# A recurrent scan with a soft mixture of experts: slot sums divided behind the experts, gates by sigmoid where the table allows, a new written order

## The chip, the cores and the metric

The kernel runs on one core of one Trainium2 chip. Such a core has a matrix engine (TensorE, PE in the profile), a vector engine (VectorE, DVE), an engine for functions of single elements (ScalarE, ACT), a general one (GpSimd, POOL) and a queue engine (SyncE, SP) from which this kernel issues all its transfers. Every engine works through its own list of instructions in order; semaphores hold an instruction back until what it needs is there. The metric is the device time of one execution in microseconds (us). PSUM, the memory into which TensorE writes, has eight banks of 128 rows by 512 numbers of four bytes here; all other tiles lie in SBUF.

## The reference

Four sequences of 5056 tokens with 256 channels go through a gated linear recurrence, and its output, as 20224 tokens, through a soft mixture of 8 experts with 4 slots each. Cut to what matters:

```python
# recurrence (B=4, S=5056, D=256), c = 8
sig_r, sig_i = sigmoid(r_gate), sigmoid(i_gate)
a_t  = exp(c * sig_r * log(clip(sigmoid(a_param), 1e-6, 1 - 1e-6)))
norm = sqrt(maximum(1 - a_t * a_t, 1e-6))
u    = norm * sig_i * x
h[t] = a_t[t] * h[t-1] + u[t]            # y = all h
# soft mixture of experts over the N = 20224 rows of y
logits = y @ phi                         # (N, 32): 8 experts x 4 slots
d = exp(logits - logits.max(0)); d /= d.sum(0) + 1e-9
slot_in = d.T @ y                        # (32, 256)
for e in range(8):                       # F = 1024
    slot_out[e] = maximum(slot_in[e] @ w1[e], 0) @ w2[e]
c = exp(logits - logits.max(1)); c /= c.sum(1) + 1e-9
out = c @ slot_out                       # (N, 256)
```

The softmax of `d` runs over all tokens, so no slot is complete before the last token has been scanned, and no output row exists before the experts are done.

## The kernel before, in words

**Windows and units.** The tokens are cut into 40 windows of 512 (the last has 256). The windows are grouped into 21 units, of one window at the start, then of two (`UNITS`, line 16). What ScalarE does on 2048 columns at once it does for a unit.

**The front of a window.** SP loads the r gate, the i gate and x (L368), tokens on the rows. TensorE turns the r gate channel-major (L383, two halves of 128 channels); ScalarE takes tanh(r/2) of each half (L393) and, for the unit, the sigmoid of the i gate (L405). GpSimd multiplies it with x (L412). Two exponentials for each unit, one for each half, make the decay a (L425): the sigmoid of r is (1 + tanh(r/2))/2, so exp(8 L sig(r)) is exp(4L tanh + 4L), and `ca`, the column with 4L (L is the logarithm of the clipped sigmoid of `a_param`), stands as scale and as bias. GpSimd squares a (L433); ScalarE takes the root of 1 minus that (L440). TensorE turns i·x channel-major (L450); VectorE multiplies it with the root (L460) and scans (L473, one for each half, each taking the last column of the window before). TensorE turns y token-major (L493), and VectorE or ScalarE copies it (L281 in the one case, L279 in the other) into one of six y tiles.

**Groups of four windows.** TensorE makes the logits (L539); VectorE copies them and takes the running maximum (L548 to L552); ScalarE makes the correction exp(old maximum - new maximum) (L557); TensorE turns logits minus maximum token-major (L563, L566), ScalarE takes their exponential (L572), TensorE multiplies it with y and a column of ones (L581, so the 257th column holds the sum of weights), and VectorE folds the result into `accS` with the correction (L590 for the first group, L592 for the others). Each of the four windows of a group has its own 32 rows of `accS`.

**From the scans to the slots.** The four row blocks have maxima of their own. L621 to L638 bring their common maximum back to the rows, L643 and L646 make the weights, L649 puts them on a pattern of identities (`Wt`). Two products then add the four blocks up (L656), and a third (L657) adds up the sums of weights, repeated on all 128 rows. VectorE adds 1e-9, takes the reciprocal and multiplies (L662 to L664): that is `slotT`, the normalised slots.

**Experts, tokens, stores.** Four pairs of experts go through L713 (first product), a copy, L725 (transposition), L731 (maximum with 0) and L740 (second product, all summed into one bank). The result is copied to `soS`, multiplied with the pattern of identities (L762), which repeats the 32 slot rows four times, and copied to `soR`. The token side makes the softmax of the logits over the slots (L790 to L810), turns it (L814), multiplies it with `soR` (L839, 32 rows at a time), copies the result (L279, L281) and stores it (L856). The expert weights come over the same SP queue (L691, L694).

**What sets the order.** All this is written as operations with a key, an engine, an estimated duration and the keys that they need. The table `ORDER` (line 25) lists the operations' numbers, a `b` marking the second of two possible engines. `Plan.order()` goes through it, books each operation on its engine by the estimated durations, and places every buffer at that point: `Plan.take` gives it one of 38 halves of 19 G pairs, six y tiles, two e tiles and eight banks, preferring what is free by the estimated times. The instructions are then emitted in the table's order. So the estimated durations order nothing by themselves, but they decide which buffer an operation gets, and thereby on what it waits.

**Tables.** ScalarE holds one table of functions at a time: exponential with tanh, sigmoid with tanh, square root, or logarithm with exponential. A function of another table makes it load one (ACT_TABLE_LOAD). The planner books 1.283 us for it (`TABLE_US`) and keeps the name of the table loaded.

## Time and profile before

| what | value |
|---|---|
| median of 3 runs | 308.71 us (307.37 to 308.96) |
| the profiled execution | 307.92 us |
| its span (first to last instruction) | 306.1 us |
| granted TensorE clock, mean | 0.928 |
| TensorE busy | 241.1 us (79%) |
| VectorE busy | 238.0 us (78%) |
| ScalarE busy | 246.1 us (80%) |
| GpSimd busy | 181.7 us (59%) |
| moved over the DMA queues | 100.03 MB, mean 327 GB/s |

How to read it: the page gives busy time by engine, then the span in 40 slices with the busy share of each engine in tenths, then the DMA queues, the chain of work that ended last, and the costliest groups of instructions. A row of a timeline reads: start, duration, engine, source line, operation, out<-in, shape, count; in brackets the idle time of the engine before it and what ended that idle time. A row of a group reads: line, engine, operation, count, then busy us and the mean of one in ns, then the idle time before the group's instructions. Lines (L440) are lines of the kernel.

### The profile page before, as it was taken

Reading aid. Unit: us, or ns where it says so; the run is one execution under the profiler, and the core shown is the slowest. Engines: PE = TensorE matmul, PEld = TensorE weight load, DVE = VectorE, ACT = ScalarE, POOL = GpSimd, SP = SyncE. Lnnn points to the kernel's source line nnn. Section 1 sums busy time; section 2 is a strip of 40 time slices with the busy share of each in tenths; the row PEclk is TensorE's granted clock in tenths of the full one; section 3 lists DMA queues with packets and bytes.
Section 4 is the critical chain, followed back from the end, with each engine's and each line's share of the span. In section 5 each row is a group of like instructions: output and inputs, shape, how many; then the busy total and the mean of one; then the engine's idle time right before and its main releaser. Section 6 shows DMA issues by size and latency. Waiting matters only on the chain.

```text
span 306.1 us, 5779 instructions
## 1 busy us (share of the span) xinstructions
PE 241.1 (79%) x2134; PEld 170.0 (56%) x2134; DVE 238.0 (78%) x370; ACT 246.1 (80%) x311; POOL 181.7 (59%) x121
## 2 busy tenths in 40 slices
PE   3605797969888896988989788878999999898900
PEld 3604665737646754766577464736563677656700
DVE  0003999699999998999999989979967869975600
ACT  5999999999999999999999999997220457874320
POOL 1389986988598899699599996991000241031000
PEclk9955999999999999799999999999999999995565
DMA  7999999967998993998856997999990019999996
GB/s 252 415 405 408 408 376 412 396 255 286 399 383 323 410 365 122 378 413 281 327 207 238 384 363 305 335 385 349 406 359 6 2 60 401 405 403 407 361 409 269
DMA packets 28032, 100.03 MB, mean 327 GB/s; under 512 B 3362, under 2 KB 3364, under 8 KB 28004
## 3 DMA queue, kind: packets, MB, share of 16 engines
q1 hardware_dynamic: 28004, 99.66, 84.8%
q8 instruction: 17, 0.28, 0.4%
q14 instruction: 11, 0.09, 0.1%
HBM read 78.94 MB, written 20.71 MB: 326 GB/s over the span
## 4 chain that ended last, share of the span: by engine, by line
PE 25%; ACT 25%; DVE 15%; issue 9%; POOL 6%; DMA 3%; ACTq 0%; SPq 0%; DVEq 0%; POOLq 0%
PE b L839 7%; ACT g L425 7%; DVE g L473 6%; ACT g L393 5%; DVE b L460 4%; ACT g L405 4%; POOL g L412 3%; ACT g L440 3%; POOL g L433 2%; DVE y L281 2%; PE b L713 2%; PE b L740 2%; PE b L493 2%; PE b L450 2%; ACT y L279 2%
## 5 line engine op out<-in xcount | busy, mean ns | idle before, releaser
L412 POOL TENSOR_TENSOR g<-g,g 128x1024 f32<-128x1024 f32 (+1 forms) x40 | 92.7, 2347 | 10.6 <-ACT g L405 10.1
L433 POOL TENSOR_TENSOR g<-g 128x1024 f32<-128x1024 f32 (+1 forms) x40 | 73.8, 1873 | 25.0 <-ACT g L425 21.9
L460 DVE SCALAR_TENSOR_TENSOR b<-g,b 128x512 f32<-128x512 f32 (+1 forms) x80 | 51.5, 677 | 31.4 <-ACT g L440 30.2
L450 PE MATMUL b<-ident,g 128*128 128x128 f32 x316 | 47.6, 286 | 21.7 <-POOL g L412 15.5
L493 PE MATMUL b<-ident,g 128*128 128x128 f32 x316 | 46.9, 283 | 10.4 <-DVE g L473 4.1
L450 PEld LDWEIGHTS b<-ident,g 128*128 128x128 f32 x316 | 35.8, 145 | 34.1 <-POOL g L412 17.7
L383 PE MATMUL b<-ident,g 128*128 128x128 f32 x316 | 46.5, 288 | 8.1 <-DMA g<-in_r_gate_dram 3.2
L473 DVE TENSOR_TENSOR_SCAN g<-g,g,b 128x512 f32<-128x512 f32 x40 | 50.3, 1271 | 0.2
L473 DVE TENSOR_TENSOR_SCAN g<-g,b 128x512 f32<-128x512 f32 (+7 forms) x46 | 49.2, 1094 | 0.3
L493 PEld LDWEIGHTS b<-ident,g 128*128 128x128 f32 x316 | 35.1, 143 | 23.7 <-DVE g L473 8.6
L425 ACT ACTIVATE g<-g,ca 128x1024 f32<-128x1024 f32 (+2 forms) x44 | 47.5, 1158 | 0.0
L810 POOL TENSOR_TENSOR y<-y,rs 128x512 f32<-128x512 f32 x10 | 10.4, 1048 | 61.3 <-DVE rs L807 59.8
L383 PEld LDWEIGHTS b<-ident,g 128*128 128x128 f32 x316 | 36.4, 146 | 18.0 <-ACT g L393 4.3
L393 ACT ACTIVATE g<-b 128x512 f32<-128x512 f32 x80 | 42.2, 605 | 2.5 <-PE b L383 2.4
L281 DVE COPY y<-b 128x512 f32<-128x512 f32 x55 | 36.4, 678 | 6.9 <-PE b L814 3.5
L405 ACT ACTIVATE g<-g 128x2048 f32<-128x2048 f32 (+2 forms) x22 | 38.2, 1755 | 0.1
L440 ACT ACTIVATE g<-g 128x2048 f32<-128x2048 f32 (+2 forms) x22 | 37.2, 1736 | 0.1
L279 ACT COPY g<-b 128x512 f32<-128x512 f32 x47 | 24.7, 593 | 14.3 <-PE b L839 13.5
L839 PE MATMUL b<-soR,y 32*128 32x256 f32 x320 | 31.2, 462 | 3.4 <-DVE y L281 2.3
L839 PEld LDWEIGHTS b<-soR,y 32*128 32x128 f32 x320 | 22.0, 219 | 10.0 <-ACT g L279 3.2
L281 DVE COPY g<-b 128x512 f32<-128x512 f32 x33 | 21.0, 680 | 5.1 <-PE b L839 4.8
L279 ACT COPY y<-b 128x512 f32<-128x512 f32 x34 | 18.7, 592 | 5.9 <-PE b L493 5.9
(83 smaller groups left out, 244.0 us busy)
## 6 DMA issues: line engine op xcount, KB each, us to landing
g<-in_x_dram SPq DMA_DIRECT2D x39, 512.0 KB, 6.7
g<-in_i_gate_dram SPq DMA_DIRECT2D x39, 512.0 KB, 8.1
out_dram<-g SPq DMA_DIRECT2D x39, 512.0 KB, 6.2
g<-in_r_gate_dram SPq DMA_DIRECT2D x38, 512.0 KB, 6.6
g<-in_moe_w_dram SPq DMA_DIRECT2D x32, 512.0 KB, 6.3
g<-in_r_gate_dram SPq DMA_DIRECT2D x3, 256.0 KB, 5.8
g<-in_i_gate_dram SPq DMA_DIRECT2D x1, 256.0 KB, 8.9
g<-in_x_dram SPq DMA_DIRECT2D x1, 256.0 KB, 8.8
```

The costliest lines, as they stand in the source:

```text
L281: nc.vector.tensor_copy(out=dst, in_=srct)
L383: nc.tensor.transpose(out=by_tile(rp, n)[:, j, :], in_=rows(("r", w), n)[:, j, h * P : (h + 1) * P], identity=ident,)
L393: nc.scalar.activation(halves(("A", w))[:, h, :c], Bk(("rp", w, h))[:, :c], AF.Tanh, scale=0.5)
L405: nc.scalar.activation(a, a, AF.Sigmoid)
L412: nc.gpsimd.tensor_tensor(out=rows(("x", w), n), in0=rows(("i", w), n), in1=rows(("x", w), n), op=ALU.mult)
L425: nc.scalar.activation(a, a, AF.Exp, scale=ca[:, h : h + 1], bias=ca[:, h : h + 1])
L433: nc.gpsimd.tensor_tensor(out=halves(("N", w))[:, :, :c], in0=a, in1=a, op=ALU.mult)
L450: nc.tensor.transpose(out=by_tile(up, n)[:, j, :], in_=rows(("x", w), n)[:, j, h * P : (h + 1) * P], identity=ident,)
L460: nc.vector.scalar_tensor_tensor(up, halves(("N", w))[:, h, :c], 1e-3, up, op0=ALU.max, op1=ALU.mult)
L473: nc.vector.tensor_tensor_scan(dst, dst, up[:, s0:s1], init, op0=ALU.mult, op1=ALU.add)
L493: nc.tensor.transpose(out=yp[:, j, h * P : (h + 1) * P], in_=halves(("A", w))[:, h, (2 * i + j) * P : (2 * i + j + 1) * P], identity=ident,)
L839: nc.tensor.matmul(Bk(("op", w0, n))[:, i * D : (i + 1) * D], hT()[r, (2 * i2 + i) * P : (2 * i2 + i + 1) * P], soR[r, :], start=True, sto ...
```

## The change

**Slot sums.** The third product at L657 is gone. `slotT` is now a plain copy of the two sums, not normalised. The maximum with 0 and the two products of an expert go through with a positive factor on a slot, so the division can stand behind them. A new operation `dn` makes four products of 32 by 1 (`Wt` with the column of sums of weights), so that the denominator of a slot stands in a column, on the rows on which the slot outputs are after the identity product; `rd` adds 1e-9 to it and takes the reciprocal, and the copy to `soR` becomes a scaling by that column, on whichever engine has it.

**Gates.** Where the planner finds the sigmoid table loaded for all gates of a unit, `plain` is true: the gate is then sigmoid(r) in place of tanh(r/2), and the exponential has `ca8`, a new column with 8L, as scale and no bias. With the new table of the order this is so for units 6, 8, 10, 14, 22 and 26 (by their first window); these hold 24 of the 80 gates and 12 of the 44 exponentials. All others keep their form.

**PSUM tiles and costs.** The list of eight one-bank tiles is renamed (`bank` to `banks`). Several estimated durations are new, and the accumulating products of the second half of a y tile now name the copy of the first half beside that of the second.

**Order.** The table is another one, with two operations more.

```diff
 ORDER = """
-1 74 96 5 33 11 115 55 13 12 34 56 75 116 4 35 219 137 57 241 97 159 301 76 138 160 98 179 201 117 2 0 6 7 8 9
...
+1 74 96 5 115 2 0 3 6 7 8 9 10 77 79 101 99 118 78 102 80 100 119 120 83 121 11 16 14 15 33 55 36 58 124 17 60
...
-            o.start, o.end = t, t + us
+            o.start, o.end, o.table = t, t + us, table
...
-    bank = [ps.tile([P, C], F32, name=f"b{i}") for i in range(8)]
+    banks = [ps.tile([P, C], F32, name=f"b{i}") for i in range(8)]
...
+    ca8 = const.tile([P, H], F32, name="ca8")
...
-    rd = const.tile([P, 1, NS], F32, name="rd")
+    rd = const.tile([P, 1], F32, name="rd")
...
     def e_decay3(o):
+        nc.vector.tensor_scalar(ca8, ca, 8.0, None, op0=ALU.mult)
         nc.vector.tensor_scalar(ca, ca, 4.0, None, op0=ALU.mult)
...
+    def plain(unit):
+        return all(plan.by_key[("sr", v, h)].table == "S" for v in unit for h in range(H))
...
-            op(("L" + nm, w), "DMA", (2.6 if (nm, w) == ("i", 0) else 1.29) * f, load(nm), alloc=gets(nm), uses=has(nm))
+            op(("L" + nm, w), "DMA", 1.29 * f, load(nm), alloc=gets(nm), uses=has(nm))
...
-                nc.scalar.activation(halves(("A", w))[:, h, :c], Bk(("rp", w, h))[:, :c], AF.Tanh, scale=0.5)
+                f, k = (AF.Sigmoid, 1.0) if plain(unit) else (AF.Tanh, 0.5)
+                nc.scalar.activation(halves(("A", w))[:, h, :c], Bk(("rp", w, h))[:, :c], f, scale=k)
...
-                    nc.scalar.activation(a, a, AF.Exp, scale=ca[:, h : h + 1], bias=ca[:, h : h + 1])
+                    if plain(unit):
+                        nc.scalar.activation(a, a, AF.Exp, scale=ca8[:, h : h + 1])
+                    else:
+                        nc.scalar.activation(a, a, AF.Exp, scale=ca[:, h : h + 1], bias=ca[:, h : h + 1])
...
             op(("acc", t, j), "PE", 0.48, e_acc(j),
-               deps=[("ee", t), ("acc", t, j - 1)] + [("yc", w, j // 2) for w in ws],
+               deps=[("ee", t), ("acc", t, j - 1)] + [("yc", w, i) for w in ws for i in {0, j // 2}],
...
     def sp():
-        return Bk(("sp",))[:, : (H + 1) * NS].rearrange("p (h s) -> p h s", s=NS)
+        return Bk(("sp",))[:, : H * NS].rearrange("p (h s) -> p h s", s=NS)
...
-        nc.tensor.matmul(
-            sp()[:, H, :], accS[:, D : D + 1].broadcast_to([P, P]), Wt, start=True, stop=True
-        )
 
     def e_slot(o):
-        nc.vector.tensor_scalar(rd, sp()[:, H : H + 1, :], 1e-9, None, op0=ALU.add)
+        nc.vector.tensor_copy(out=slotT, in_=sp())
+
+
+    def e_dn(o):
+        for j in range(J):
+            nc.tensor.matmul(
+                Bk(("dn",))[32 * j : 32 * j + NS, :1], Wt, accS[:, D : D + 1], start=True, stop=True
+            )
+
+    def e_rd(o):
+        nc.vector.tensor_scalar(rd, Bk(("dn",))[:, :1], 1e-9, None, op0=ALU.add)
         nc.vector.reciprocal(rd, rd)
-        nc.vector.tensor_tensor(out=slotT, in0=sp()[:, :H, :], in1=rd.broadcast_to([P, H, NS]), op=ALU.mult)
...
     def e_s2(o):
-        copy(o, soR, Bk(("sr",))[:, :D])
+        if o.on == "ACT":
+            nc.scalar.activation(soR, Bk(("sr",))[:, :D], AF.Copy, scale=rd)
+        else:
+            nc.vector.tensor_scalar(soR, Bk(("sr",))[:, :D], rd, None, op0=ALU.mult)
...
-    op(("s2",), ("DVE", "ACT"), {"DVE": 0.34, "ACT": 0.28}, e_s2, deps=[("s1",)], uses=[("sr",)])
+    op(("s2",), ("DVE", "ACT"), {"DVE": 0.34, "ACT": 0.28}, e_s2, deps=[("s1",), ("rd",)], uses=[("sr",)])
```

In the lists that follow, `g`, `y`, `e` and `b` with a number are the G halves, y tiles, e tiles and banks as the planner placed them; `m`, `n`, `d` are running maxima, their negatives and the corrections, `rm` the maxima over a token's slots. Lines after the change are those of the new file, some 5 to 20 higher.

ScalarE, the fourth of the seven stretches that take square roots. Before (L440 root, L279 copy of y, L405 sigmoid):

```order
L425 ACTIVATE g_64<-g_64,ca 128x2x512 x2
L440 ACT_TABLE_LOAD
L440 ACTIVATE g_79<-g_79 128x2048
L279 COPY y_81<-b_95 128x2x256
L440 ACTIVATE g_65<-g_65 128x2048
L279 COPY y_85<-b_89 128x2x256
L279 COPY y_81<-b_93 128x2x256
L279 COPY y_82<-b_90 128x2x256
L279 COPY y_83<-b_94 128x2x256
L440 ACTIVATE g_73<-g_73 128x2048
L405 ACT_TABLE_LOAD
L405 ACTIVATE g_68<-g_68 128x2048
```

The same stretch after the change (L449 root, L280 copy, L411 sigmoid, L566 correction factor, L400 gate):

```order
L566 ACTIVATE d_145<-m_122,n_134 128x1
L280 COPY y_81<-b_91 128x2x256
L400 ACTIVATE g_71<-b_88 128x512
L449 ACT_TABLE_LOAD
L449 ACTIVATE g_74<-g_74 128x2048
L449 ACTIVATE g_67<-g_67 128x2048
L449 ACTIVATE g_62<-g_62 128x2048
L280 COPY y_83<-b_93 128x2x256
L411 ACT_TABLE_LOAD
L411 ACTIVATE g_73<-g_73 128x2048
```

The three roots stand behind each other, two copies of y stand here in place of five, one of them ahead of the table load with a correction and a gate.

VectorE where the slots are made. Before (L592 folds a group in, L649 the weights, L662 to L664 the slots, L796 the first step of the token side):

```order
L592 SCALAR_TENSOR_TENSOR accS<-accS,d_150,b_94 128x257
L592 SCALAR_TENSOR_TENSOR accS<-accS,d_152,b_90 32x257
L649 SCALAR_TENSOR_TENSOR Wt<-R,wj 128x32
L592 SCALAR_TENSOR_TENSOR accS<-accS,d_151,b_88 96x257
L662 TENSOR_SCALAR rd<-b_91 128x32
L663 RECIPROCAL rd<-rd 128x32
L664 TENSOR_TENSOR slotT<-b_91,rd 128x64
L796 TENSOR_REDUCE rm_155<-b_88 128x16
```

After (L640 the common maximum, L652 and L658 the weights, L601 the folding in, L668 the slots, L816 the token side):

```order
L816 TENSOR_REDUCE rm_158<-b_92 128x16
L640 TENSOR_REDUCE mmax<-b_95 1x32
L601 SCALAR_TENSOR_TENSOR accS<-accS,d_151,b_90 128x257
L652 TENSOR_TENSOR wj<-m_130,b_93 128x1
L658 SCALAR_TENSOR_TENSOR Wt<-R,wj 128x32
L601 SCALAR_TENSOR_TENSOR accS<-accS,d_152,b_89 96x257
L601 SCALAR_TENSOR_TENSOR accS<-accS,d_153,b_91 32x257
L668 COPY slotT<-b_91 128x64
L816 TENSOR_REDUCE rm_156<-b_93 128x16
```

The slots take one instruction in place of three, and the weights stand ahead of two foldings in place of one.

TensorE behind the experts. Before (L740 second product of the experts, L814 a transposition of the token side, L762 the product with the identities, L790 the next token transposition, L839 the first store product):

```order
L740 MATMUL b_90<-g_73,g_74 32x256 x4
L740 MATMUL b_90<-g_68,g_74 32x256 x4
L740 MATMUL b_90<-g_63,g_74 32x256 x4
L814 MATMUL b_91<-ident,y_84 128x128 x4
L762 MATMUL b_90<-soS,R 128x256
L790 MATMUL b_94<-ident,l_102 128x4x32 x4
L839 MATMUL b_95<-soR,y_84 128x256
```

After (L757, L834, L779, L810 and L859 are those lines; L673 is the denominator):

```order
L757 MATMUL b_92<-g_70,g_62 32x256 x4
L757 MATMUL b_92<-g_69,g_62 32x256 x4
L757 MATMUL b_92<-g_61,g_62 32x256 x4
L673 MATMUL b_90<-accS,Wt 32x1 x4
L834 MATMUL b_91<-ident,y_83 128x128 x4
L779 MATMUL b_92<-soS,R 128x256
L810 MATMUL b_90<-ident,l_102 128x4x32 x4
L859 MATMUL b_91<-soR,y_83 128x256
L859 MATMUL b_92<-soR,y_83 128x256
```

The four products of the denominator stand between the last expert's product and the transposition, and the first store products have other banks.

More of the change, by code (lines that the diff above doesn't have):

```diff
@@ L73 @@
+1140 1214 1192 1207 1141 1147
 """
@@ L228, in Bk @@
     def Bk(key):
-        return bank[plan.place[key]]
+        return banks[plan.place[key]]
     def rows(key, n):
@@ L399, in window @@
             op(("sr", w, h), "ACT", 0.05 + 0.43 * f, e_sr(h), deps=[("rp", w, h)],
-               alloc=gets("A") if h == 0 else [], uses=[("rp", w, h)] + ([("A", w)] if h or not first else []),
-               act="ES")
+               alloc=gets("A") if h == 0 else [], uses=[("rp", w, h)] + ([("A", w)] if h or not first else []), act="ES")
         def e_si(o):
```

87 lines of the change are left out of this document (44 added, 43 removed), and 30 rows, old and new, of the table ORDER.

## The prediction

> **What bounds the kernel now.** I read the slices of the page first, then the waits of VectorE, then its and ScalarE's timelines around the end of the scans.
>
> ```profile
> ACT  5999999999999999999999999997220457874320
> DVE  0003999699999998999999989979967869975600
> GB/s 252 415 405 408 408 376 412 396 255 286 399 383 323 410 365 122 378 413 281 327 207 238 384 363 305 335 385 349 406 359 6 2 60 401 405 403 407 361 409 269
> ```
>
> A slice is 7.65 us. ScalarE is full to slice 26, about 207 us; VectorE, busy from slice 3, nearly so. Then memory stands still for two slices (6 and 2 GB/s, 230 to 245 us: the experts), and from slice 33 to the end it moves some 400 GB/s: the 40 stores, bound by memory. So the kernel is gates and scans (ScalarE), a chain through the slots and experts, and a store stage whose length is fixed; what counts is when it starts.
>
> ```profile
> DVE b L460 <- ACT g L440: 30.2, 5, 23.9
> ```
>
> ```profile
> 61.10 1.29 DVE L460 SCALAR_TENSOR_TENSOR b<-g,b 128x512 f32<-128x512 f32 x2 [1.64 <-ACT g L440]
> ...
> 119.75 1.29 DVE L460 SCALAR_TENSOR_TENSOR b<-g,b 128x512 f32<-128x512 f32 x2 [1.32 <-ACT g L440]
> ...
> 177.60 0.69 DVE L460 SCALAR_TENSOR_TENSOR b<-g,b 128x512 f32<-128x512 f32 x1 [1.13 <-ACT g L440]
> ...
> 205.44 1.29 DVE L460 SCALAR_TENSOR_TENSOR b<-g,b 128x512 f32<-128x512 f32 x2 [2.26 <-ACT g L440]
> ```
>
> ```profile
> 202.21 1.28 ACT L440 ACT_TABLE_LOAD   x1
> 203.50 1.91 ACT L440 ACTIVATE g<-g 128x2048 f32<-128x2048 f32 x1
> 205.32 1.06 ACT L279 COPY y<-b 128x512 f32<-128x512 f32 x2
> ```
>
> VectorE waits five times for a square root (L440): once at the start, then 1.64, 1.32, 1.13 and 2.26 us. The last one decides. The root of windows 36 and 37 ends at 205.41; VectorE, idle since 203.18, starts on them at 205.44 and has the four last windows to scan. So the term that sets the scans' end is ScalarE's work ahead of that root, and VectorE is 2.26 us behind it as second bound.
>
> ```profile
> 218.90 0.75 DVE L473 TENSOR_TENSOR_SCAN g<-g,b 128x256 f32<-128x256 f32 x1
> ```
>
> **The change, part by part.** *ScalarE's list.* Ahead of that root the new order has the same 80 gates, 21 sigmoids, 21 groups of exponentials, 19 roots and the same number of table loads, but 15 copies of y in place of 17, and 7 correction factors (L557) in place of 6. Two copies took 1.06 us above. With the price of a factor from the fence below (0.285) that is 1.06 - 0.285 = 0.8 less; I take 0.7, since neighbours overlap, with 0.5 and 0.9 as ends.
>
> *Exponentials without a bias.* Six pairs of windows (6, 8, 10, 14, 22, 26) get their gates while the sigmoid table is loaded; their twelve exponentials then have a column as scale and a plain 0 as bias, where all had two columns.
>
> ```profile
> L425 ACT ACTIVATE g<-g,ca 128x512 f32<-128x512 f32 x6 | 4.7, 834 | 0.0
> ...
> L557 ACT ACTIVATE d<-m,n 128x1 f32<-128x1 f32 x8 | 2.3, 285 | 0.0
> ...
> L405 ACT ACTIVATE g<-g 128x512 f32<-128x512 f32 x1 | 0.7, 660 | 0.0
> ...
> L646 ACT ACTIVATE wj<-wj 128x1 f32<-128x1 f32 x1 | 0.2, 203 | 1.5 <-DVE wj L643 1.5
> ```
>
> Exponentials of one element a row take 285 ns with a column as bias and 203 without: 82 ns. At 512 elements the one with two columns takes 834, a sigmoid with none 660: 174 ns, or 87 each. Twelve times 0.085 is 1.0 us less. The ends: nothing, if the column of the scale alone costs all of it, and 2.1 us (12 x 0.174) if the bias does. The Trainium skill has a price too (ScalarE: Activation LUTs, What ACT_TABLE_LOAD costs): each column operand adds about 93 ns and the function itself makes no difference; by it the gain would be 1.1 us, and it also speaks against one piece of the change, since the scaling behind the experts gets such an operand where a plain copy had none. The trace's 82 and 87 ns agree with it.
>
> *Sigmoid for tanh* in the 24 gates of these windows:
>
> ```profile
> L393 ACT ACTIVATE g<-b 128x512 f32<-128x512 f32 x78 | 41.5, 609 | 2.5 <-PE b L383 2.4
> ...
> L572 ACT ACTIVATE e<-b 128x512 f32<-128x512 f32 x9 | 5.4, 598 | 0.1
> ```
>
> Tanh and exponential of 512 elements out of a bank are 11 ns apart, so the function hardly shows: 24 x 0.011 is 0.3 us either way; I take 0. The extra column (one VectorE instruction among the decay's, before any scan) is hidden under the first loads: VectorE's slices are empty there. The PSUM tiles only get another name; there were eight one-bank tiles, and there are.
>
> So the root of windows 36 and 37 should end 0.7 + 1.0 = 1.7 us earlier, at 203.7. **Does VectorE keep up?** It now has 52 copies ahead of that point, not 48, and one more 257-wide accumulation.
>
> ```profile
> 139.79 2.46 DVE L281 COPY y<-b 128x512 f32<-128x512 f32 x4
> ```
>
> Four copies take 2.46 us, the accumulation under half a microsecond: 2.8 more. It was there at 203.18; with nothing else changed it would be there at 206.0, and if its waits for earlier roots (1.64 + 1.32 + 1.13 = 4.1) all went, at 201.9. Every root comes earlier by its part of the 1.7, so I take 203.5: level with ScalarE. The scans' end moves by **-1.6** (ends: +0.5 by VectorE, -2.9 by the largest price of a bias).
>
> *From the scans to the experts.*
>
> ```profile
> 227.55 0.63 PE L656 MATMUL b<-Wt,accS 128*128 128x32 f32 x4
> ...
> 228.01 0.39 PE L657 MATMUL b<-Wt,accS 128*128 128x32 f32 x2
> ...
> 228.44 0.19 DVE L662 TENSOR_SCALAR rd<-b 128x32 f32<-128x32 f32 x1 [0.95 <-PE b L657]
> 228.67 0.35 DVE L663 RECIPROCAL rd<-rd 128x32 f32<-128x32 f32 x1
> 229.05 0.22 DVE L664 TENSOR_TENSOR slotT<-b,rd 128x64 f32<-128x64 f32 x1
> ...
> 229.36 1.14 PE L713 MATMUL b<-g,slotT 128*32 128x512 f32 x8
> ```
>
> The third product (L657) ends at 228.40; without it the slots are ready when L656 ends, 228.18. VectorE's three instructions take 0.83 us (228.44 to 229.27); one copy of the last one's size takes 0.22. Together 0.22 + 0.61: **-0.8** (ends -0.4 and -1.1). The rest of that stretch has the same chain of maxima, weights and accumulations in both orders, so I give it nothing.
>
> *Behind the experts.* The denominator is now four small products, recorded as eight, on TensorE between the last expert and a transposition that is ahead of the slot output's product.
>
> ```profile
> 225.14 0.24 PE L638 MATMUL b<-ones,mmax 1*32 1x1 f32 x8
> ```
>
> ```profile
> 246.41 0.37 ACT L279 COPY soS<-b 128x256 f32<-128x256 f32 x1 [5.18 <-PE b L740]
> ...
> 246.84 0.70 PE L762 MATMUL b<-soS,R 128*128 128x256 f32 x2
> ...
> 246.97 0.69 DVE L281 COPY y<-b 128x512 f32<-128x512 f32 x1 [2.04 <-PE b L814]
> ...
> 247.57 0.37 ACT L279 COPY soR<-b 128x256 f32<-128x256 f32 x1 [0.79 <-PE b L762]
> ...
> 248.00 1.15 PE L839 MATMUL b<-soR,y 32*128 32x256 f32 x16
> ...
> 250.55 24.63 SPq L856 DMA_DIRECT2D out_dram<-g  x21
> ```
>
> The nearest small products are those of L638: eight in 0.24 us. L762 waited for the transposition and the copy alike (246.78 to 246.84), so it moves by that 0.24. On VectorE the sum and reciprocal of the denominator (at most 0.19 + 0.35) stand ahead of the copy that ended at 247.66, and the first store product was ready at 248.00: 0.34 of slack. With a column on ScalarE's scaling (0.08) I take **+0.3**; ends 0 and +0.8. From the first store (250.55) to the end, 55.6 us, nothing changes: 20.7 MB at some 405 GB/s is 51.
>
> **Sum:** -1.6 - 0.8 + 0.3 = -2.1 us. The profiled execution took 307.92 (span 306.1 and 1.8 around it), which is 0.79 under the median of the runs, 308.71. So 305.8 for its like, and **306.6** as a median.
>
> **Rivals.** *VectorE takes over (308.2).* If its 2.8 us more are not repaid by earlier roots, the scans start 0.5 later: +0.5 - 0.8 + 0.3 = 0, 308.7 at worst; half repaid, 308.2. For it: its slices of 9. Against: 4.1 us of waits to give up. It decides if VectorE reaches windows 36 later than 203.7.
>
> *Loads just in time (311.7, slower).* The order of the reads and the buffers that they take are new.
>
> ```profile
> 81.97 0.43 SPq L368 DMA_DIRECT2D g<-in_i_gate_dram  x1
> ```
>
> ```profile
> 90.58 1.06 PE L539 MATMUL b<-g,phi_sb 128*32 128x512 f32 x8
> ```
>
> ```profile
> 101.78 1.96 ACT L405 ACTIVATE g<-g 128x2048 f32<-128x2048 f32 x1
> ```
>
> ```profile
> g<-in_i_gate_dram SPq DMA_DIRECT2D x39, 512.0 KB, 8.1
> ```
>
> The i gate of window 21 was issued at 81.97, for a sigmoid at 101.78: 20 us ahead. In the new order it and that of window 20 take buffers last read by the logits of windows 8 to 11 (L539, done at 91.64 here), with two loads between them. A load takes 8.1 us in the median: landing at 99.7, or with the loads ahead of it 103.5, 1.7 us late. ScalarE then stands, and with it everything. Once costs 1.7 and leaves 308.3; in three of the six later rounds 5.1: 311.7. It decides from 3.6 us of such waits (306.6 + 3.6 is 0.5% over 308.71). For it: the queue waits for buffers often. Against: ScalarE shows no such wait between 12 and 205 us now, and those logits can come earlier too, as nothing in their list has grown.
>
> *The last weight load is late (307.6).*
>
> ```profile
> 222.51 0.43 SPq L691 DMA_DIRECT2D g<-in_moe_w_dram  x1
> ```
>
> The load issued last now belongs to the second pair of experts to be multiplied; in the new order to experts 0 and 1, also second, behind a stage that comes 2.4 us earlier. If it keeps its time, 8 us after 222.51 is 230.5, and those products, due at 228.8 (229.36 - 2.4 + 1.8), lose up to 1.7: about 1.0 of it gives 307.6.
>
> **How the numbers follow.** Forecast 0.5, VectorE 0.18, late loads 0.2, late weights 0.12. 0.5% of 308.71, about what a measurement of this kernel can tell from no change, is 1.5 us: faster means under 307.2. The forecast lies there with 0.45 of its 0.5 (its own range is 305.3 to 307.6), late weights with 0.02; single late loads (0.03), the rest of the weights (0.1), of the forecast (0.05) and VectorE (0.15) are no change, 0.33; late loads from three rounds on and a VectorE that falls further behind are slower, 0.2. The range is 304.8 (the bias at its largest price) to 310.8, two late rounds past the forecast and some.
>
> **What would show it.** The root of windows 36 and 37 should end near 203.7 and VectorE wait under a microsecond for it; exponentials of L432 should be some 85 ns shorter than those of L434; from the last scan to the first expert product 9.7 us should become 8.9; from that product to the first store 21.2 should become 21.5; the stores should take 55.6 again. Idle time of ScalarE before L400 or L411 put down to a DMA would prove the forecast wrong, as would a VectorE without any wait for roots.

## The result: 304.27 us, and the profile after

The changed kernel takes 304.27 us in the median of 4 runs (303.24 to 304.64), the kernel before 308.31 of 4 on that occasion: a ratio of 0.9866, interval 0.9828 to 0.9904. In the next comparison it was 304.37 against 307.91, 0.9884 (0.9856 to 0.9911). So it is faster, by 1.3 and 1.2%. The forecast was faster, but by half of that: 306.6, and the range ended at 304.8, above the result.

Both profiled executions cut at the same five events, in us; each number is the difference of two rows that stand here or in the prediction, rounded last:

| stretch | before | after | moved | forecast |
|---|---|---|---|---|
| start to the end of the root of windows 36, 37 | 205.41 | 204.30 | -1.11 | -1.7 |
| to the end of the last scan | 14.23 | 13.62 | -0.61 | +0.1 |
| to the first expert product | 9.71 | 8.46 | -1.25 | -0.8 |
| to the end of the last expert product | 16.98 | 17.24 | +0.26 | 0 |
| to the first store | 4.21 | 4.31 | +0.10 | +0.3 |
| to the end of the span | 55.54 | 54.72 | -0.82 | 0 |
| span | 306.1 | 302.65 | -3.4 | -2.1 |

The row of the page with the memory's traffic in 40 slices, now of 7.57 us, and the one of VectorE's waits for the root:

```profile
GB/s 250 332 417 409 402 409 409 408 303 262 409 408 324 416 267 277 406 136 375 376 355 291 254 369 368 343 403 384 330 371 7 2 50 402 405 398 408 372 413 299
```

```profile
DVE b L469 <- ACT g L449: 25.6, 4, 23.5
```

The picture is the same one: two slices of nothing for the experts, then some 400 GB/s to the end. Four waits are left of five, and after the first, 23.5, they come to 2.1 us where they were 6.3. The rows of the change at the five events, from the timelines of ScalarE, VectorE, TensorE and the store queue (start, duration, engine, line, operation; in brackets the idle time before):

```profile
202.38 1.92 ACT L449 ACTIVATE g<-g 128x2048 f32<-128x2048 f32 x1
```

```profile
204.33 1.29 DVE L469 SCALAR_TENSOR_TENSOR b<-g,b 128x512 f32<-128x512 f32 x2 [1.30 <-ACT g L449]
...
216.54 1.38 DVE L482 TENSOR_TENSOR_SCAN g<-g,b 128x256 f32<-128x256 f32 x2
...
225.94 0.23 DVE L668 COPY slotT<-b 128x64 f32<-128x64 f32 x1 [0.89 <-PE b L665]
...
243.78 0.16 DVE L678 TENSOR_SCALAR rd<-b 128x1 f32<-128x1 f32 x1 [2.76 <-PE b L673]
```

```profile
226.38 3.64 PE L730 MATMUL b<-g,slotT 128*32 128x512 f32 x32
...
238.23 5.39 PE L757 MATMUL b<-g,g 128*32 128x256 f32 x96
243.44 0.22 PE L673 MATMUL b<-accS,Wt 128*32 128x1 f32 x8
```

```profile
247.93 49.52 SPq L876 DMA_DIRECT2D out_dram<-g  x40
```

The last expert product of before, for the fourth and fifth stretch, ended at 246.35:

```profile
240.96 5.39 PE L740 MATMUL b<-g,g 128*32 128x256 f32 x96
```

The root ends at 204.30 and VectorE still waits for it, 1.30 us where it was 2.26. The slots are one copy, and the first expert product follows it by 0.2. The denominator's eight recorded products take 0.22, where the forecast had 0.24. What the forecast did not have: the scans behind the last root are 0.6 shorter, and the stores are 0.8 shorter.

The exponentials by form, in the change:

```profile
L434 ACT ACTIVATE g<-g,ca 128x1024 f32<-128x1024 f32 x24 | 28.3, 1246 | 0.0
L432 ACT ACTIVATE g<-g,ca 128x1024 f32<-128x1024 f32 x12 | 12.9, 1144 | 0.0
```

One column less is 102 ns, for 85 forecast. That is the size for which the prediction named the Trainium skill (ScalarE: Activation LUTs, What ACT_TABLE_LOAD costs): 93 ns for each column; the trace is 9 above it. That the function makes no difference agrees too: the 80 gates (L400) take 597 ns in the mean in the change and 599 in e1 below, where all of them are tanh.

### The profile page after: what moved, and what is told of

Same layout as the page of the kernel before. It is cut to its first block, busy times and chain, and to the rows that moved or that the text cites. A ratio compares the mean times of both kernels' runs of the same rounds, so it can differ in the third digit from the quotient of the medians.

```text
span 302.6 us, 5773 instructions
## 1 busy us (share of the span) xinstructions
PE 240.0 (79%) x2140; PEld 168.5 (56%) x2140; DVE 241.4 (80%) x378; ACT 241.8 (80%) x304; POOL 182.0 (60%) x121
## 4 chain that ended last, share of the span: by engine, by line
DVE 26%; PE 23%; ACT 16%; DMA 12%; issue 9%; POOL 7%; SPq 1%; ACTq 0%; DVEq 0%; POOLq 0%
DVE g L482 10%; DMA g<-in_r_gate_dram 7%; DVE b L469 5%; PE b L388 5%; DMA g<-in_i_gate_dram 4%; ACT g L400 4%; POOL g L442 4%; ACT g L434 4%; DVE g L282 4%; POOL g L418 3%; PE b L859 3%; DVE y L282 3%; PE b L730 2%; PE b L757 2%; PE b L548 2%
## 5 line engine op out<-in xcount | busy, mean ns | idle before, releaser
L418 POOL TENSOR_TENSOR g<-g,g 128x1024 f32<-128x1024 f32 (+1 forms) x38 | 88.3, 2347 | 19.9 <-ACT g L411 17.6
L459 PE MATMUL b<-ident,g 128*128 128x128 f32 x316 | 48.9, 289 | 19.7 <-POOL g L418 14.6
L388 PE MATMUL b<-ident,g 128*128 128x128 f32 x316 | 50.3, 305 | 9.0 <-DVE g L482 5.0
L459 PEld LDWEIGHTS b<-ident,g 128*128 128x128 f32 x316 | 36.6, 147 | 32.3 <-POOL g L418 21.0
L502 PE MATMUL b<-ident,g 128*128 128x128 f32 x316 | 46.0, 280 | 6.3 <-DVE g L482 4.5
L388 PEld LDWEIGHTS b<-ident,g 128*128 128x128 f32 x316 | 40.2, 157 | 18.3 <-DVE g L482 8.3
L502 PEld LDWEIGHTS b<-ident,g 128*128 128x128 f32 x316 | 34.6, 142 | 20.3 <-DVE g L482 8.3
L400 ACT ACTIVATE g<-b 128x512 f32<-128x512 f32 (+1 forms) x80 | 43.3, 597 | 3.1 <-PE b L388 2.7
L282 DVE COPY y<-b 128x512 f32<-128x512 f32 x60 | 39.5, 676 | 2.2 <-PE b L502 1.3
L411 ACT ACTIVATE g<-g 128x2048 f32<-128x2048 f32 (+2 forms) x22 | 38.2, 1744 | 0.1
L449 ACT ACTIVATE g<-g 128x2048 f32<-128x2048 f32 (+2 forms) x22 | 37.1, 1736 | 0.1
L434 ACT ACTIVATE g<-g,ca 128x1024 f32<-128x1024 f32 (+2 forms) x32 | 33.7, 1127 | 0.0
L280 ACT COPY g<-b 128x512 f32<-128x512 f32 x46 | 24.4, 596 | 10.7 <-PE b L859 9.7
L859 PE MATMUL b<-soR,y 32*128 32x256 f32 x320 | 27.9, 404 | 3.2 <-ACT g L280 1.1
L859 PEld LDWEIGHTS b<-soR,y 32*128 32x128 f32 x320 | 18.5, 183 | 10.0 <-ACT g L280 3.8
L590 PE MATMUL b<-y,e 128*32 128x257 f32 x316 | 22.4, 385 | 0.6 <-ACT e L581 0.4
```

Of the source, the lines that this page charges most:

```text
L282: nc.vector.tensor_copy(out=dst, in_=srct)
L388: nc.tensor.transpose(out=by_tile(rp, n)[:, j, :], in_=rows(("r", w), n)[:, j, h * P : (h + 1) * P], identity=ident,)
L400: nc.scalar.activation(halves(("A", w))[:, h, :c], Bk(("rp", w, h))[:, :c], f, scale=k)
L411: nc.scalar.activation(a, a, AF.Sigmoid)
L418: nc.gpsimd.tensor_tensor(out=rows(("x", w), n), in0=rows(("i", w), n), in1=rows(("x", w), n), op=ALU.mult)
L434: nc.scalar.activation(a, a, AF.Exp, scale=ca[:, h : h + 1], bias=ca[:, h : h + 1])
```

## The experiments

All numbers of a profiled execution by the same cuts (root is its end in us; the others are lengths), medians of all runs, and ratios to the kernel before with their intervals:

| run | median | ratio | root | to last scan | to experts | experts | to store | stores |
|---|---|---|---|---|---|---|---|---|
| before | 307.64 to 308.31 | 1 | 205.41 | 14.23 | 9.71 | 16.98 | 4.21 | 55.54 |
| change (c0) | 304.37 | 0.9884 (0.9856, 0.9911) | 203.92 | 13.62 | 8.46 | 17.24 | 4.31 | 54.70 |
| e1 | 304.79 | 0.9891 (0.9868, 0.9914) | 204.78 | 13.62 | 8.46 | 17.24 | 4.31 | 54.59 |
| e2 | 304.54 | 0.9893 (0.9863, 0.9923) | 206.04 | 13.62 | 9.14 | 17.25 | 4.21 | 54.82 |
| e3 | 306.07 | 0.9930 (0.9907, 0.9953) | 205.27 | 13.62 | 9.15 | 17.25 | 4.21 | 54.79 |
| e4 | 306.39 | 0.9966 (0.9945, 0.9987) | 203.59 | 14.23 | 9.72 | 16.98 | 4.21 | 55.13 |
| e5 | 308.50 | 1.0047 (1.0023, 1.0071) | 205.16 | 14.23 | 9.50 | 16.92 | 5.25 | 55.11 |
| e6 | 307.20 | 0.9994 (0.9980, 1.0007) | 206.75 | 14.23 | 9.72 | 16.99 | 4.21 | 54.78 |
| e7 | 305.34 | 0.9919 (0.9894, 0.9943) | 203.65 | 13.62 | 8.47 | 17.24 | 4.31 | 55.59 |
| e8 | 307.99 | 1.0006 (0.9984, 1.0027) | 205.90 | 14.68 | 9.52 | 16.98 | 4.21 | 55.90 |
| e9 | 307.64 | 0.9997 (0.9974, 1.0019) | 205.02 | 14.23 | 9.50 | 16.91 | 4.31 | 55.72 |
| e10 | 308.29 | 1.0023 (1.0005, 1.0041) | 203.53 | 17.17 | 8.74 | 17.25 | 4.31 | 55.20 |
| e11 | 304.10 | 0.9873 (0.9849, 0.9896) | 202.75 | 13.62 | 8.46 | 17.24 | 4.31 | 54.82 |
| e12 | 308.04 | 1.0005 (0.9981, 1.0028) | 206.77 | 13.62 | 10.78 | 16.99 | 4.21 | 54.87 |
| e13 | 305.20 | 0.9892 (0.9853, 0.9931) | 203.36 | 14.90 | 8.46 | 17.24 | 4.32 | 54.82 |

Read down a column: the four middle stretches repeat to 0.02 us from execution to execution where the code is the same, while medians of single kernels differ by half a microsecond from chance. A stretch of the profile tells 0.1 us apart here; a median of six runs does not tell 0.4. The root's end and the stores are the two columns that scatter.

**The change again, and its two edits undone.** c0 is the change once more; e1 puts the tanh gates and two columns back, e2 the division ahead of the experts (L657 and L662 to L664 of before in place of the copy, `dn` and `rd` empty), e3 both.

```diff
 def plain(unit):
-    return all(plan.by_key[("sr", v, h)].table == "S" for v in unit for h in range(H))
+    return False
```

> The changed kernel once more, beside the others on the same chip. If the sum of parts is right and the rest of the difference between the two first profiles is spread of single executions, the ratio to the kernel before stays near 304.3/308.3 = 0.987, and the stretch from the first store to the end, 54.7 us in the first profile of the change and 55.6 in that of before, comes out anywhere between the two. If the new order made the store stage shorter, it is 54.7 again.

> The changed kernel with tanh gates and two columns in all exponentials again (order, buffers and slots as in the change). Sum of parts: the profile of the change has 1144 ns for an exponential with one column and 1246 with two, so twelve cost 1.2 us more; ScalarE has no gap to take that up, the root of windows 36 and 37 ends near 205.5 instead of 204.3, VectorE's wait for it grows from 1.30 to 2.5 us and the time is 1.2 us above the changed kernel's. Rival (VectorE sets the pace now, the gates were worth nothing): within 0.4 us of the changed kernel.

> The changed kernel with the division ahead of the experts again (third product, three VectorE instructions, plain copy behind the experts; the denominator's operations emit nothing; order and buffers as in the change). Sum of parts: 0.22 for the third product and 0.61 for two VectorE instructions more ahead of the experts, 0.3 less behind them: 0.5 us above the changed kernel; from the last scan to the first expert product 8.46 becomes 9.3. Rival (the last expert weights, or the two foldings that now stand behind the weights, set that start): 8.5 again, and the time 0.3 us under the changed kernel's.

> Both undone: tanh gates with two columns and the division ahead of the experts, so the new order, costs and buffers alone. Sum of parts: 1.2 + 0.5 = 1.7 us above the changed kernel and 2.3 below the kernel before. Rivals: the order is worth nothing by itself (the time of the kernel before), or it is worth all (the changed kernel's time within 0.5 us).

c0 and e3 came as expected: 54.70 us of stores again, and 306.07 us for the order alone, 1.70 above c0. The medians of e1 and e2 did not: 0.42 above c0 for 1.2 expected, which is about the rival's 0.4, and 0.17 for 0.5. In e1 the root ends at 204.78, not at 205.5, and VectorE's wait for it is not 2.5 us but 1.30. It is 1.30 in the change, c0, e1, e2 and e3 alike, though the root ends anywhere from 203.92 to 206.04. So what VectorE does ahead of that wait moves with ScalarE. The parts do not add in medians of five or six runs; what each is worth is read from the stretches.

The division is worth what the pair of profiles says: 9.14 against 8.46 ahead of the experts and 4.21 against 4.31 behind them, so 0.58 net, with or without the gates. In the timeline of e3 (the order alone), VectorE:

```profile
227.14 0.19 DVE L671 TENSOR_SCALAR rd<-b 128x32 f32<-128x32 f32 x1 [1.11 <-PE b L666]
227.37 0.35 DVE L672 RECIPROCAL rd<-rd 128x32 f32<-128x32 f32 x1
227.76 0.22 DVE L673 TENSOR_TENSOR slotT<-b,rd 128x64 f32<-128x64 f32 x1
```

These rows stand where the change has its one copy. The root's end scatters by what ScalarE waits ahead of it, 4.1 to 6.0 us in the profiles (gaps over 0.15 us). Without those waits its list up to the root's end comes to 201.1 us in the old order with tanh (mean of six profiles), 200.5 in the new order with tanh (e1, e3) and 199.7 in the new order with the gates (four): 0.6 for the order and 0.8 for the gates. Twelve times the 102 ns of a column would be 1.2; what became of the rest is not shown. e3 as a whole took 306.07, so order, costs and buffers alone are a gain of 0.7%.

e2 also shows the rival of loads just in time. Its profiled execution, 306.93, is 2.4 above its own median, and ScalarE's timeline has

```profile
22.40 2.86 ACT L411 ACTIVATE g<-g 128x1024 f32<-128x1024 f32 x2 [0.42 <-DMA g<-in_i_gate_dram]
...
32.68 1.28 ACT L411 ACT_TABLE_LOAD   x1 [0.51 <-DMA g<-in_i_gate_dram]
...
44.68 1.91 ACT L411 ACTIVATE g<-g 128x2048 f32<-128x2048 f32 x1 [0.95 <-DMA g<-in_i_gate_dram]
```

1.9 us of waits for the i gate, at 22, 33 and 45 us rather than at 100 where the forecast looked. None of the seven other profiles of the new order has a wait of ScalarE for a load behind the first 12 us. So the hazard is there, seen in one execution.

**The gates alone, the division alone, on the kernel before.** e4 has the gates in the old order, where by that order seven units have them (14 exponentials). e5 has the division in the old order; the two operations were put right behind the last expert:

```diff
 # the order's numbers, as keys
  so,3
+ dn
+ rd
  c2,0    (VectorE: a token group's sum and reciprocal)
  s0
  ...
  hx,1    (VectorE: the copy that the first store product needs)
```

> The kernel before with the gate change alone, in its own order: by that order seven units (6, 10, 16, 22, 24, 34, 38) have all gates in the sigmoid table, six of them ahead of the last root. Sum of parts, with the sums of ScalarE's work in the first profiles (45.0 against 46.1 us of exponentials for twelve): 12 to 14 exponentials at 0.09 is 1.1 to 1.3 us; the last root ends at 204.2 instead of 205.4 and the time falls by 1.1. Rival (the gain needs the new order, since in the old one VectorE or the loads hold the scans): the root comes earlier but VectorE's wait of 2.26 us stays or the scans end where they did, under 0.4 us.

> The kernel before with the division moved behind the experts, alone: two operations are added to its order behind the last expert, all else where it was. By the pair of profiles with and without it in the new order (9.14 against 8.46 us from the last scan to the first expert product, 4.21 against 4.31 from the last expert to the first store): 9.71 becomes 9.0, 4.21 becomes 4.3, and the time falls by 0.6. Rival (the folding that stands behind the weights in the old order sets the start): 9.7 stays.

e4 did what was expected and a little more: the root ends at 203.59, the time fell by 1.25, and the new order was not needed for it (ScalarE's list, without its waits, is 199.5 in e4 and e10: 1.6 off 201.1 for 14 exponentials). e5 made the kernel slower, where a gain of 0.6 was expected. Ahead of the experts only 0.21 came, and behind them 1.04 was lost. The timelines of VectorE and of TensorE in e5:

```profile
227.97 0.23 DVE L659 COPY slotT<-b 128x64 f32<-128x64 f32 x1 [0.72 <-PE b L656]
...
245.97 0.16 DVE L669 TENSOR_SCALAR rd<-b 128x1 f32<-128x1 f32 x1 [2.98 <-PE b L664]
246.16 0.17 DVE L670 RECIPROCAL rd<-rd 128x1 f32<-128x1 f32 x1
246.24 0.67 DVE L816 TENSOR_REDUCE rs<-y 128x16 f32<-128x512 f32 x1
...
247.32 0.63 DVE L281 COPY y<-b 128x512 f32<-128x512 f32 x1
```

```profile
227.77 1.19 PE L801 MATMUL b<-ident,l 128*128 128x128 f32 x8
228.89 1.49 PE L721 MATMUL b<-g,slotT 128*32 128x512 f32 x12
```

The same place on TensorE in before:

```profile
228.24 1.19 PE L790 MATMUL b<-ident,l 128*128 128x128 f32 x8
```

In e5 the slots are ready at 228.20, but TensorE is in two token transpositions until 228.9. In before they ran beside VectorE's three instructions and cost nothing; with these gone, the transpositions set the start. Behind the experts VectorE stands 2.98 us before the denominator, with the token group behind it, and the copy for the first store product comes at 247.32 where before had it at 246.97 (and here the experts end 0.5 earlier).

e9 moves `rd` behind that token group and changes nothing else:

```diff
  so,3
  dn
- rd
  c2,0
  ...
+ rd
  hx,1
```

> The division alone in the old order, as in the run before it, with one thing changed: VectorE's sum and reciprocal of the denominator stand behind a token group's sum and reciprocal, not ahead of them. In the run before, VectorE stood 2.98 us before the denominator's product with that group behind it, and the copy that the first store product needs came at 247.32; the stretch from the last expert to the first store grew from 4.21 to 5.25. If that queue is the cause, the stretch is 4.3 here; from the last scan to the first expert product 9.5 stays (two token transpositions stand on TensorE between the slot sums and the experts), and the time is 0.1 us under the kernel before, 0.9 under the run before. Rival (the scaling or the four products themselves cost the 1 us): 5.2 again.

```profile
245.82 0.16 DVE L669 TENSOR_SCALAR rd<-b 128x1 f32<-128x1 f32 x1 [1.59 <-PE b L664]
246.02 0.16 DVE L670 RECIPROCAL rd<-rd 128x1 f32<-128x1 f32 x1
246.32 0.69 DVE L281 COPY y<-b 128x512 f32<-128x512 f32 x1
```

The stretch is 4.31, as in the change, and the time that of the kernel before. So the four products and the scaling cost 0.1; the other 0.94 was the queue.

**The store stage.** e6 is the kernel before up to its first store product and the order of the change (with its cost of 1.35 for a store product) from there; e7 the reverse.

```diff
 # e6: the order's numbers
  old order, up to the first op (L839)
- old order, op to the last out
+ new order, op to the last out
```

> The kernel before up to its first store product, with the store stage in the order of the change (both orders have the same operations done by then). From the first store to the end before takes 55.54 us, the new order 54.6 to 54.8 in five profiles. If the order of the store stage makes that difference, this has 54.7, the spread of the last packets' ends falls from 1.07 to about 0.5 us and the time falls by 0.8. Rival (spread between executions of the memory, or the half clock of TensorE that fell on that stage in the profile of before): 55.5 in the one execution as in the next where the clock is halved, and no gain in the median.

> The reverse of the run with the new store stage on the old kernel: the changed kernel up to its first store product, then the store stage in the old order. If the order of that stage is worth what four profiles of the old (55.1, 55.1, 55.5, 55.9; the two longer ones with TensorE's clock at one half inside it) and six of the new order (54.6 to 54.8) say, it takes 55.1 here, or 55.5 to 55.9 if the clock is halved before its products end, and the time is 0.4 to 1.1 us above the changed kernel's. Rival (what goes before it makes the difference): 54.7.

The stage has 54.78 us in e6 and 55.59 in e7, as expected. The times say less. e6's is not told from that of before: its interval ends at 0.9980, which is a gain of 0.6 us, so the expected 0.8 is not there. (Its profiled execution lost 1.25 us to a wait at 38 us.) e7 is about 1 us above the change, but the two intervals overlap. And TensorE's clock was halved in the stage of e7 and not in that of e6, so the two differ in more than the order. Over all profiles the stage's length goes with two things. TensorE's granted clock is the third number from the right in these rows, each a window of one profile's store stage: before, e9, e7, e10 (where it falls), e5 and the change (where it does not). The row's first numbers are the window, its length, and busy time and instructions of TensorE, its weight loads, VectorE, ScalarE and GpSimd; the last two are the share of the DMA engines and GB/s.

```profile
276.00:289.00 13.00, 11.36 (x85) 8.84 (x87) 7.16 (x14) 5.41 (x11) 1.05 (x1) 0.50 1.02 380
```

```profile
275.00:288.60 13.60, 11.56 (x87) 9.00 (x90) 7.64 (x14) 5.83 (x12) 1.05 (x1) 0.50 1.02 379
```

```profile
264.80:271.60 6.80, 6.80 (x49) 4.70 (x52) 5.65 (x13) 3.58 (x7) 2.45 (x3) 0.50 1.00 392
```

```profile
268.00:275.00 7.00, 7.00 (x44) 4.37 (x45) 4.74 (x10) 3.78 (x8) 1.05 (x1) 0.52 1.02 401
```

```profile
251.00:288.00 37.00, 32.59 (x348) 23.29 (x348) 31.77 (x60) 26.07 (x51) 5.24 (x6) 1.00 0.99 387
```

```profile
268.00:287.00 19.00, 13.26 (x144) 9.09 (x143) 14.23 (x26) 11.22 (x22) 2.05 (x2) 1.00 1.02 391
```

| store stage | clock full until the last product | clock halved within it |
|---|---|---|
| old order | 54.87, 55.11, 55.13 (e12, e5, e4) | 55.54, 55.59, 55.72, 55.90 (before, e7, e9, e8) |
| new order | 54.59 to 54.82 (eight profiles) | 55.20 (e10) |

Old against new with a full clock is some 0.3 us; with the halved clock the stage is 0.4 to 0.9 longer. Where these differences arise, the memory's traffic tells. Three pairs of rows, for before, the change and e8: from 2 us after the first store to 5 us before the end, then the last 5 us.

```profile
252.55:301.09 48.54, 34.62 (x324) 25.17 (x317) 30.77 (x58) 26.40 (x51) 5.20 (x5) 0.77 1.02 398
301.09:306.09 5.00, 0.00 (x0) 0.00 (x0) 0.00 (x0) 0.00 (x0) 0.00 (x0) 0.50 0.50 197
```

```profile
249.93:297.65 47.72, 30.59 (x326) 21.40 (x322) 31.77 (x59) 26.56 (x51) 5.20 (x5) 0.89 1.02 400
297.65:302.65 5.00, 0.00 (x0) 0.00 (x0) 0.00 (x0) 0.00 (x0) 0.00 (x0) 0.50 0.61 243
```

```profile
253.28:302.18 48.90, 36.01 (x324) 25.95 (x317) 30.78 (x58) 26.50 (x51) 5.19 (x5) 0.75 0.99 387
302.18:307.18 5.00, 0.00 (x0) 0.00 (x0) 0.00 (x0) 0.00 (x0) 0.00 (x0) 0.50 0.68 270
```

In before the halved clock did not starve the stores: up to the last 5 us the DMA engines are as full as in the change (1.02) and move nearly as much (398 and 400 GB/s). The difference is in the last 5 us, when no engine of the core works any more and one DMA engine after the other comes to its end. They are busy for 0.50 of that time in before and for 0.61 in the change; 0.11 of 5 us is 0.55 of the 0.82. Over the other profiles the share goes with the stage's length: 0.59 to 0.63 in the new order with a full clock, 0.52, 0.54 and 0.59 in the old one (e5, e4, e12), 0.53 in e10, 0.49 and 0.47 in e7 and e9. The ends of the last 16 packets lie 0.98 us apart in before and 0.34 in e6. Only in e8 is the traffic clearly lower ahead of the end (0.99, 387 GB/s), and there the engines end together. Why the order, or the clock, makes the DMA engines end unevenly is not shown.

The halved clock falls on the old order more often. Every run has a mean clock beside its time. Of 82 executions of the kernel before, 37 have a mean under 0.935, with a median of 308.47, the other 45 307.62. Of 63 executions of the six other kernels with the old store order 21 are under 0.935, of 63 with the new one 5. Neither part is an experiment of its own: the order's 0.3 compares three profiles with eight, the clock's part executions that fell one way or the other. The mean clock does not say where in the span it was low, and whether it lengthens the stage or goes with something else that does stays open.

**From the last root to the last scan.** The work is the same in both orders: eight products (L460) and eight scans. In before, four scans stand directly behind the product whose result they read; in the change none. VectorE in before:

```profile
211.83 0.68 DVE L460 SCALAR_TENSOR_TENSOR b<-g,b 128x512 f32<-128x512 f32 x1
212.54 1.28 DVE L473 TENSOR_TENSOR_SCAN g<-g,b 128x512 f32<-128x512 f32 x1
```

The scan starts 0.71 after the product. e8 changes the sequence, and e12 in addition puts a transposition (L450) ahead of three logit products:

```diff
 # e8: VectorE, windows 37 to 39
- st37,0 sc37,0 st37,1 sc37,1 st38,0 sc38,0 st38,1 st39,0 sc38,1 sc39,0 st39,1 sc39,1
+ st37,0 st37,1 sc37,0 st38,0 sc37,1 sc38,0 st38,1 st39,0 sc38,1 st39,1 sc39,0 sc39,1
 # e12, beside it: TensorE
- lp9,0  up39,1
+ up39,1 lp9,0
```

> The kernel before, with VectorE's products and scans of the windows 37 to 39 in another sequence: no scan stands directly behind the product whose result it reads (in before four of the last do; a scan then starts 0.71 to 0.78 us after the product's start, where another instruction starts 0.58 after it). If that is why the stretch from the last root to the last scan went from 14.23 to 13.62 us, it is 13.7 here and the time falls by 0.5. Rival (it is work that went to ScalarE, or TensorE's transpositions): 14.2 stays.

> The earlier run with another sequence of VectorE's last products and scans once more, with one thing changed: the transposition for the second half of window 39 stands ahead of three logit products on TensorE and not behind them (VectorE waited 0.95 us for it there). If the distance between a product and the scan that reads it is what the change gained from the last root to the last scan, that stretch is 13.7 here (14.23 in before, 14.68 with the wait); the wait is gone and the time is 0.5 below the kernel before. Rival (VectorE is held by TensorE there in any sequence of the old order): another wait, and 14.2 or more.

VectorE in e8, and then in e12:

```profile
212.78 0.68 DVE L460 SCALAR_TENSOR_TENSOR b<-g,b 128x512 f32<-128x512 f32 x1
213.36 1.27 DVE L473 TENSOR_TENSOR_SCAN g<-g,b 128x512 f32<-128x512 f32 x1
...
218.85 0.43 DVE L460 SCALAR_TENSOR_TENSOR b<-g,b 128x256 f32<-128x256 f32 x1 [0.95 <-PE b L450]
```

```profile
219.01 1.38 DVE L473 TENSOR_TENSOR_SCAN g<-g,b 128x256 f32<-128x256 f32 x2
220.87 0.75 DVE L549 TENSOR_SCALAR_CACHE_REDUCE l<-b,m 96x512 f32<-96x512 f32 x1 [0.47 <-PE b L539]
```

In e8 the distance is 0.58, and a wait of 0.95 for TensorE ate the gain. In e12 that wait is gone and the stretch is 13.62, the number of the change to the hundredth: the distance explains this stretch. But the logits now come later (0.47 of wait in the row above), the next stretch is 10.78 in place of 9.71, and the time is that of before, not 0.5 below it. In that the rival was right: TensorE makes another wait. A gap that is closed on one engine has to be closed with the others in step; the new order did that, the two small edits did not.

**Joining, and going further.** e10 takes the old order with the gates up to the last root and the new one with the division from there. e11 chooses the gate for each half of a unit. e13 is e11 with one y copy ahead of the last root on VectorE.

```diff
 # e11
-def plain(unit):
-    return all(plan.by_key[("sr", v, h)].table == "S" for v in unit for h in range(H))
+def plain(unit, h):
+    return all(plan.by_key[("sr", v, h)].table == "S" for v in unit)
 # e13, in the order: yc,31,1 from ScalarE to VectorE
```

> Both joined: the old order with the new gates up to the last root (seven units with sigmoid gates, that root at 203.6 in its profile against 203.9 and 204.3 in two of the change), from there the new order with the division behind the experts. Sum of parts: 203.6 + 13.62 + 8.46 + 17.24 + 4.31 + 54.7 = 301.9 us of span, 0.5 under the changed kernel (302.2 to 302.6), about 303.9 as a median. Rival (the pieces fit badly: buffers or expert weights are late where one order goes over into the other): a stretch grows and the time is over 304.4.

> The changed kernel, where the choice between sigmoid and tanh is made for each half of a unit and not for the whole: four more exponentials go with one column (three of them halves of units 12, 18, 38, the last in two pieces), 0.09 us each. Sum of parts: the last root 0.3 earlier and the time 0.3 us lower, which the medians may not tell apart; the sum of ScalarE's exponentials falls from 45.03 to 44.7. Rival (the price is in something else than the bias column): the same sum.

> The changed kernel with the choice of gate for each half (as in the run for that) and one of ScalarE's copies of y ahead of the last root (window 31) on VectorE. ScalarE's list is 0.53 shorter ahead of that root and VectorE's 0.6 longer, out of a wait of 1.1 us. If the two engines are the two bounds as the waits show them, the root ends 0.5 earlier than in the run without this (by the same idle time), VectorE's wait is near nothing, and the time is 0.3 to 0.5 under that run's 304.1. Rival (the copy comes at a point where VectorE is late already, so the scans move with it): the same time or more.

e10 went the rival's way, 308.29 us for 303.9 expected. Where one order goes over into the other a correction factor comes behind the root, with a table load of its own, and VectorE stands 4.45 us for it (VectorE, then ScalarE):

```profile
206.12 0.48 DVE L601 SCALAR_TENSOR_TENSOR accS<-accS,d,b 128x257 f32<-128x257 f32 x1 [4.45 <-ACT d L566]
```

```profile
204.50 1.28 ACT L566 ACT_TABLE_LOAD   x1
205.80 0.29 ACT L566 ACTIVATE d<-m,n 128x1 f32<-128x1 f32 x1
```

e11 has the earliest root of all, 202.75, and the lowest median, 304.10, but the interval of its ratio overlaps that of the change: it is not shown to be better. (The sum of its exponentials, counts times means of the forms, fell by 0.1 us for 0.3 expected.) e13 went the rival's way too, 305.20 us where about 303.7 was expected: the copy stands behind a wait for TensorE, and VectorE reaches the root's windows late:

```profile
194.65 0.69 DVE L282 COPY y<-b 128x512 f32<-128x512 f32 x1 [1.23 <-PE b L502]
...
203.93 0.67 DVE L282 COPY y<-b 128x512 f32<-128x512 f32 x1
204.51 1.29 DVE L469 SCALAR_TENSOR_TENSOR b<-g,b 128x512 f32<-128x512 f32 x2
```

No idle time before the product: VectorE is the bound there, 1.15 us behind a root that ended at 203.36. In the change ScalarE sets the pace, with VectorE 1.3 us ahead; one copy moved across was enough to turn that round.

## Why the prediction was wrong, point by point

From 306.6 to 304.27 there are 2.33 us. In the profiled executions the forecast was 305.8, the result 304.51: 1.3 of it. The other 1.0 is the step from one execution to the median.

- **"0.79 under the median of the runs ... and 306.6 as a median".** This step failed. Three runs gave 308.71; in the five comparisons the kernel before had 308.31, 307.91, 307.64, 307.77 and 307.98, and the profiled 307.92 lies in the middle of them. The change's profile was 0.24 above its median. An offset that was chance was carried on as if it belonged to the kernel.
- **"From the first store (250.55) to the end, 55.6 us, nothing changes".** This step failed, by 0.82. The bytes are the same, and up to the last 5 us the traffic nearly is; but the DMA engines end less evenly in before (busy for 0.50 of the last 5 us against 0.61). The stage's length goes with the order of its work, some 0.3, and with TensorE's clock, 0.4 to 0.9 where it was halved, as in before and not in the change. What joins these to the uneven end stays open. The row of the page of before that shows the halved clock, its 5s ahead of the last product at 290.84:

```profile
PEclk9955999999999999799999999999999999995565
```

- **"The rest of that stretch has the same chain ... so I give it nothing".** Mis-sized. From the last scan to the experts the order alone gave 0.56 (9.71 to 9.15), and the division 0.69 where 0.8 was forecast. In the old order the division gives 0.21, since transpositions fill its place (e5, e9). By VectorE's timelines in before and e3, counted from the last scan's end, the new order is 0.2 ahead at the common maximum (L631, L640), 0.4 at the weights (L643, L652) and 0.5 where the slots begin (L662, L671). Which of its moves does it was not tested.
- **ScalarE's list, -0.7 and -1.0.** Nearly right in size: 0.6 and 0.8 with the waits taken off, from six, two and four profiles. That the root came 1.11 earlier and not 1.4 in the first pair is the scatter of those waits.
- **VectorE "level with ScalarE", and +0.1 from there to the last scan.** VectorE was 1.3 us ahead, over the microsecond that the forecast allowed; e13 shows what one more wait on that side does. The stretch behind the root became 0.61 shorter, since no scan stands directly behind its product any more, which the forecast did not see. That the scans' end moved by -1.73 for -1.6 forecast is luck: the root gave less, and these 0.61 made up for it.
- **Behind the experts, +0.3.** 0.10 in its place, and 0.26 within the experts that was forecast as nothing (the same in e3, so it belongs to the order). TensorE's timeline shows where: before has eight products of the experts' transpositions (L725) in a row in 1.23 us, the change two times four (L742) in 0.75 each. That the sum from the first expert product to the first store is 21.55 us for 21.5 forecast is luck as well. The warning that belongs here is e5's 1.04: the same instructions, with the wait three instructions earlier in VectorE's list.
- **The rivals.** VectorE taking over: not in the change, shown in e13. Late weights: no, TensorE has no gap over 0.15 us from the first expert product to the denominator in the change. Loads just in time: once in eight profiles of that order, 1.9 us.

On the range: its lower end, 304.8, took the largest price of a bias and the offset; nothing in it stood for a shorter store stage or shorter scans, which were taken as fixed.

## What to carry to other kernels

Compare two profiles stretch by stretch between fixed events: equal code repeats to a few hundredths of a microsecond there, while medians of a handful of runs scatter by half a microsecond, and a term forecast as zero is found at once. Do not give a stage bound by memory a change of nothing because its bytes are the same: look at how evenly its transfers end, and beside it at the granted clock. A new wait goes as far back in its engine's list as the use of its result allows (e5 and e9). And before an instruction is taken off the path, look at what another engine does beside it: that work may set the time next (e5).

## What the runs showed of the hardware

By the trace's records of the clock, TensorE's was halved in the middle of a stage in which it was at work: for 13.65 us from 275.7 in before, 13.65 in e9, 17.1 in e8 and 6.8 in e7 and e10, all multiples of 3.41 us. The Trainium skill (TensorE: Matmul & The Clock Gate, What's actually happening) has that window, 3413 ns, and halves the clock after an idle one. The window's length agrees; idle it was not: in the 3.41 us ahead of the halving TensorE is busy for 2.4 to 3.3 us, and 18 products start in before, 19 in e9, 22 in e8 and e10, 25 in e7, where most windows of the stage have 28 to 42. The count alone does not decide: windows with 18 in e5 and e12, and with 21 to 23 in e4, c0, e1 and e11, were not followed by it.

VectorE starts an instruction 0.58 to 0.61 us after the start of a 512-column product (recorded at 0.67 to 0.70) when it does not read that product's result, and 0.71 to 0.78 after it when it does. The Trainium skill (VectorE: DVE Perf Modes, The DRAIN you can't avoid) says that the next instruction does not start until the pipeline is empty, that a semaphore between the two costs nothing extra, and that an instruction that is not held starts earlier. Here 0.10 to 0.20 us depend on whether the neighbour's result is read. Whether the semaphore or the pipeline costs that was not told apart.
